# Channel mixing in two 64-row halves, placed between the score matmuls of each pair of heads

## The chip, the cores and the metric

The kernel runs on one core of one Trainium2 chip. The metric is the device time of one execution in microseconds (us), as the median of several runs. The engines are named as the profile names them: PE is the matrix engine and PEld its weight loads, DVE the vector engine, ACT the scalar engine with its activation functions, POOL the general engine, SP the engine that issues most DMAs. Every engine works through its own instructions in program order and waits on semaphores for the others. PSUM is the memory that matmuls write to.

## What is computed

Cosine attention over 8 batches, 12 heads, 448 positions and 64 elements a head, then a mixer block on the attention's output. Cut to what matters:

```
q_n, k_n = q / (norm(q) + 1e-6), k / (norm(k) + 1e-6)
attn = softmax(q_n @ k_n.T / tau) @ v                  # per head
x    = attn as [8, 448, 768]                           # heads side by side
u    = x + (relu(x.T @ w_tok1) @ w_tok2).T             # token mixing, 448 -> 256 -> 448
out  = u + relu(u @ w_ch1) @ w_ch2                     # channel mixing, 768 -> 1536 -> 768
```

## The kernel before, in words

**The work.** The attention is cut into 48 pairs of heads: 8 batches of 6 pairs. For pair i, `squares` (POOL), `norm_sum` (DVE), `norm_root` (two small ACT instructions), `norm_rec` (two small DVE instructions) and `normalize` (POOL) give normalised q and k in fp16, and `tpose_dma` lets a DMA of SP's queue transpose them into `qkT`. `score(i, g)` (L261) then makes two of the four score tiles of the pair: for each tile two matmuls, one per head, of 64 rows each, in the lower and the upper half of the array's rows; they write the two banks of a tile `pS`, of which there are two. `expo` (L268, ACT) takes the exponential of one score tile. `pv(i - 1, half)` (L282) multiplies the previous pair's exponentials by v: 24 small matmuls for the first three token tiles and 8 for the last; DVE divides by the sums (L288, L289).

**The mixer of a batch** is a list of jobs. `tok1` (L313; relu on ACT, L316) and `tok2` (L326 and, for the token tile that two batches share, L331; DVE adds x, L335) are the token mixing, called "front". When both halves of a token tile of u are there, it is cast to fp16, by DVE for tiles 1 and 5 (`recast`, L127) and by ACT for the others (L341), and a DMA transpose on SP's queue (L342) writes it to `uT`. `ch1(ct)` (L381) is the first channel mixing: 6 matmuls, each over all token tiles of `uT`, 384 columns in even batches and 512 in odd ones, and a relu on ACT into `gT` (L384). `ch2(i, dh)` (L397) is the second: 12 matmuls of 128 rows by 384 columns that add up in one PSUM tile `pF`, which DVE then adds to u (L401); `store` sends a finished token tile out.

**The order.** Slots 0 to 12 (`opening`) have an order of their own. From slot 13 on, `slot(i)` issues: squares, score group 0 and its two exponentials, `fill`, the norm's sum and root, `pv` first part, `fill`, score group 1 and its two exponentials, `fill`, the norm's reciprocal, normalisation and transpose, the cast of v, `fill`, `pv` second part, `fill`. Each `fill` takes mixer jobs from the list `todo` as far as a credit allows; `spread` sets that credit so that the jobs of a batch last six slots. After every sixth slot a new mixer is made: its front is interleaved with the `ch2` jobs (`held`) of the mixer before, and its `ch1` jobs follow. The tiles pR, pU, pG, pF and pO all come from one PSUM pool `ps` of four buffers, given out in turn: a fifth tile waits until the first was read. After slot 48 only mixer work is left.

Of the kernel before, what the change touches and what calls it, by code (L numbers as in the profile page):

```python
# [9 lines left out]
FP32 = mybir.dt.float32  # L10
FP16 = mybir.dt.float16
AF = mybir.ActivationFunctionType
ALU = mybir.AluOpType
# [5 lines left out]
def _bcast_free(ap: bass.AP, n: int) -> bass.AP:  # L19
    return bass.AP(tensor=ap.tensor, offset=ap.offset, ap=list(ap.ap) + [[0, n]])  # L20
# [3 lines left out]
def kernel(  # L24
# [19 lines left out]
    nc = tc.nc  # L44
# [7 lines left out]
    DT, CT, TT = D // 128, C // 128, T // 128  # L52
    DH = 384
    NDH = D // DH
    NPAIR = H // 2
# [8 lines left out]
    mix = ctx.enter_context(tc.tile_pool(name="mix", bufs=1))  # L64
    ps = ctx.enter_context(tc.tile_pool(name="ps", bufs=4, space=bass.MemoryType.PSUM))
# [5 lines left out]
        name=nc.get_next_instruction_name(), act_func_set_id=ACT_SET_LN_EXP,  # L71
# [18 lines left out]
    wc2t = cst.tile([128, CT, D], FP16, name="wc2t")  # L90
# [65 lines left out]
    N = len(pairs)  # L156
# [25 lines left out]
    def small(i, nm):  # L182
        if nm not in st_[i]:
            st_[i][nm] = att.tile([P, 2, 2 * NCH], FP32, name=nm, tag=nm)
        return st_[i][nm]
# [3 lines left out]
    def norm_sum(i, j=BOTH):  # L189
        nc.vector.tensor_reduce(out=small(i, "ssq")[:, j], in_=st_[i]["sq"][:, j], axis=AXX.X,  # L190
                                op=ALU.add)

    def norm_root(i, j=BOTH):
        nc.scalar.activation(out=small(i, "ln")[:, j], in_=small(i, "ssq")[:, j], func=AF.Ln)
        nc.scalar.activation(out=nns[i % 3][:, j, :, 0], in_=small(i, "ln")[:, j], func=AF.Exp,
                             scale=0.5)
# [29 lines left out]
    def tpose_dma(i):  # L226
        s = st_[i]
        s["T"] = att.tile([128, 2, S], FP16, name="qkT", tag="qkT")
        nc.sync.dma_start_transpose(
            out=s["T"][:].rearrange("d j (c p) -> d (j c) p", c=NCH),  # L230
            in_=s["qkn"][:].rearrange("p j c g e -> p (j c g e)"))
# [34 lines left out]
    def expo(i, c):  # L266
        s = st_[i]
        nc.scalar.activation(out=s["p"][:, c], in_=s["pS"][c][:, :, 0:S], func=AF.Exp,  # L268
                             scale=inv_tau)

    def pv(i, half):
        b, pj = pairs[i]
        s = st_[i]
        xt = x16[b // 2]
        d0 = 2 * pj * E
        ts = (3,) if half else (0, 1, 2)
        pO = ps.tile([128, len(ts), 2, E + 1], FP32, name="pO", tag="ps")
        for n, t in enumerate(ts):
            c0 = 128 * t if t < 3 else S - 128
            for h in range(2):  # L280
                for c in range(NCH):
                    nc.tensor.matmul(pO[:, n, h, :], s["p"][:, c, h, c0:c0 + 128],  # L282
                                     s["v16"][:, NCH * h + c, 0:E + 1],
                                     start=(c == 0), stop=(c == NCH - 1))
        m0, hp = (64, 64 * (b % 2)) if half else (0, 0)
        nr, t0 = 128 - m0, (3 if half else 4 * (b % 2))
        rec = att.tile([128, len(ts), 2], FP32, name="rec", tag=f"rec{half}")
        nc.vector.reciprocal(out=rec[m0:128], in_=pO[m0:128, :, :, E])  # L288
        nc.vector.tensor_tensor(  # L289
            out=xt[hp:hp + nr, t0:t0 + len(ts), d0:d0 + 2 * E].rearrange(  # L290
                "p t (h e) -> p t h e", h=2),
            in0=pO[m0:128, :, :, 0:E], in1=_bcast_free(rec[m0:128], E), op=ALU.mult)
# [4 lines left out]
    def mixer(b):  # L297
        e, g = b % 2, b // 2
        xt = x16[g]
        t0, nt = (0, 3) if e == 0 else (3, 4)  # L300
        W = nt * 128
# [1 line left out]
        u32 = mix.tile([128, nt, D], FP32, name="u32", tag="u32", bufs=2)  # L303
        u16 = mix.tile([128, nt, D], FP16, name="u16", tag="u16")
        uT = mix.tile([128, DT, W], FP16, name="uT", tag="uT")
        gT = mix.tile([128, CT, W], FP16, name="gT", tag="gT")

        def tok1(tt, dh):
            def job():
# [76 lines left out]
        def ch1(ct):  # L386
            return 6 * W / 2400, partial(ch1_part, ct, 0, DT)

        def ch2(i, dh):
            def job():  # L390
                end = b == B - 1 and i == t0 + nt - 1
                parts = 2 if end and dh == NDH - 1 else 1
                for z in range(parts):
                    cols = slice(dh * DH + z * DH // parts, dh * DH + (z + 1) * DH // parts)
                    pF = ps.tile([128, DH // parts], FP32, name="pF", tag="ps")
                    for ct in range(CT):
                        nc.tensor.matmul(pF[:], gT[:, ct, (i - t0) * 128:(i - t0 + 1) * 128],  # L397
                                         wc2t[:, ct, cols],
                                         start=(ct == 0), stop=(ct == CT - 1))
                    o = u32[:, i - t0, cols]  # L400
                    nc.vector.tensor_tensor(out=o, in0=pF[:], in1=o, op=ALU.add)  # L401
                    if end:
                        store(i, cols, end)
                if dh == NDH - 1 and not end:
                    store(i, slice(0, D), end)
            return 1.96, job

        def store(i, cols, end):
            if i == 3:
                parts = [(h, 64 * h, S - 64, 64) for h in range(2)]  # L410
            else:
                f0 = 128 * (i % 4)
                parts = [(e, f - f0, f, n) for f, n in f_segments(f0, f0 + 128)]
            for z, (h, m, f, n) in enumerate(parts):
                rows = out[2 * g + h].rearrange("(p c) d -> c p d", c=NCH)
                queue = nc.scalar if end and z else nc.sync
                queue.dma_start(out=rows[f // P, f % P:f % P + n, cols],
                                in_=u32[m:m + n, i - t0, cols])

        if b == 0:  # L420
            front = (tok1_pair, tok2_pair, u_pair, ch1_part)
        else:
            front = [tok1(tt, dh) for dh in range(NDH) for tt in range(TT)]
# [4 lines left out]
    def merge(a, b):  # L428

        if not b:  # L430
            return list(a)
        r, n = [], 0
        for m, x in enumerate(b):
            while n * len(b) < (m + 1) * len(a) and n < len(a):
                r.append(a[n])
                n += 1
            r.append(x)
        return r + list(a[n:])


    todo, held, first = [], [], []
    credit, gap = [0.0], [0.0]

    def fill():
        credit[0] += gap[0]
        while todo and credit[0] > 0:
            cost, job = todo.pop(0)
            credit[0] -= cost
            job()

    AHEAD = 5
    FIRST = 2 * NPAIR + 1
# [89 lines left out]

    def slot(i):

        if i + 3 < N:
            squares(i + 3)
        if i in wide:
            wide[i]()
        if i < N:
            score(i, 0)  # L550
            expo(i, 0)
            expo(i, 1)
        fill()
        if i + 2 < N:
            norm_sum(i + 2)
            norm_root(i + 2)
        pv(i - 1, 0)
        fill()
        if i < N:
            score(i, 1)  # L560
            expo(i, 2)
            expo(i, 3)
        fill()
        if i + 2 < N:
            norm_rec(i + 2)
            normalize(i + 2, False)
            tpose_dma(i + 2)
        if i + 1 < N:
            v_cast(i + 1, i % (2 * NPAIR) == 2)
        fill()  # L570
        pv(i - 1, 1)
        fill()

    def spread(jobs, slots):
# [4 lines left out]
    for i in range(N + 1):  # L579
        if i + AHEAD < N:  # L580
            load(i + AHEAD)
        if i == 2:
            first.extend(mixer(0))
        if i < N and i % (2 * NPAIR) == 0:
            xt = mix.tile([128, 7, D], FP16, name="x16", tag="x16", bufs=2)
            x16[i // (2 * NPAIR)] = xt
            nc.vector.memset(xt[64:128, 3, :], 0.0)
        if i < FIRST:
            opening(i)
        else:  # L590
            if i == FIRST:
                normalize(i + 1, False)
                tpose_dma(i + 1)
            slot(i)
        if i == NPAIR:
            spread([(1.6, lambda: None)] + first[1][2:10], NPAIR)
            late, held = first[1][10:], first[2]
        elif i and i % NPAIR == 0:
            front, c1, c2 = mixer(i // NPAIR - 1)
            if (i // NPAIR) % 2:  # L600
                mid = merge(front, held[:-3]) + held[-3:]
            else:
                mid = front[:6] + held[:1] + front[6:9] + held[1:2] + front[9:] + held[2:]
            spread(late + mid + c1, NPAIR)
            late = []
            held = c2
    for _, job in todo + held:
        job()

# [34 lines left out]
```

## Time and profile before

| | |
|---|---|
| three runs | 401.47, 403.29 and 405.5 us; median 403.29 |
| the profiled execution | 402.3 us; its span, first to last instruction, 400.5 us |
| mean granted TensorE clock | 0.996 |
| busy | PE 379.6, ACT 263.8, DVE 233.0, POOL 194.6 us |
| first `pF` matmuls / last score group / last matmul starts about | 83 / 338.9 / 397 us of the span |

In the lines of the profile, "L261 PE MATMUL pS<-qkT 64*112 64x448 f16" is a matmul of line 261 that writes pS from qkT, with weights of 64 rows and 112 columns and a moving operand of 64x448. Behind the number of instructions stand the busy time and the mean duration of one in ns. In a timeline a row holds equal instructions that follow each other: start, length from the first start to the last end, engine, line, shapes, count. Matmuls are pipelined, so a length overlaps with the next row; the time that a row takes on PE is read from its start to the start of the next one.

### The profile page before, as it was taken

What the parts mean: (1) busy time and instruction counts of PE and PEld (TensorE: products, weight loads), DVE (VectorE), ACT (ScalarE), POOL (GpSimd) and SP (SyncE); (2) the same over time, 40 slices, a digit from 0 to 9 for tenths busy, and PEclk for the clock granted to TensorE, in tenths of its full rate; (3) what the DMA queues carried; (4) which work ended last, traced back from release to release, by engine and by line L of the source; (5) the groups of instructions that cost most, each with busy time, mean ns of one, the idle gap of its engine ahead of it and who ended that gap; (6) DMA issues with size and microseconds to landing.
All of it is one profiled execution on the core that took longest, in us unless ns stands there. A gap on an engine that the chain in (4) does not pass through costs nothing.

```text
span 400.5 us, 9027 instructions
## 1 busy us (share of the span) xinstructions
PE 379.6 (95%) x3604; PEld 218.0 (54%) x3604; DVE 233.0 (58%) x531; ACT 263.8 (66%) x455; POOL 194.6 (49%) x205
## 2 busy tenths in 40 slices
PE   2788999899999999999999999999999999999996
PEld 1455656455445555555445565565555555655454
DVE  5879988576544865467544765557634763161022
ACT  6799899864876657866677557776686666522400
POOL 3989989827454547444744546544744520000000
PEclk9989999999999999999999999999999999999999
DMA  8999999967943797548863698547971452035014
GB/s 221 252 260 248 202 268 253 246 154 192 232 96 93 174 214 205 156 117 174 220 173 92 153 186 243 132 115 175 252 161 41 77 135 77 2 78 120 0 41 118
DMA packets 97465, 63.57 MB, mean 159 GB/s; under 512 B 57552, under 2 KB 93968, under 8 KB 97424
## 3 DMA queue, kind: packets, MB, share of 16 engines
q1 hardware_dynamic: 94048, 58.14, 59.7%
q0 software_dynamic: 3184, 4.72, 6.7%
q8 instruction: 28, 0.46, 0.5%
q10 hardware_dynamic: 192, 0.15, 0.1%
q14 instruction: 13, 0.11, 0.1%
HBM read 43.38 MB, written 11.01 MB: 136 GB/s over the span
## 4 chain that ended last, share of the span: by engine, by line
PE 84%; DVE 9%; ACT 4%; DMA 1%; issue 1%
PE pF L397 28%; PE pG L381 27%; PE pO L282 10%; PE pS L261 10%; PE pR L313 5%; PE pU L326 3%; DVE ssq L190 3%; ACT pE L268 2%; DVE x L289 2%; DVE qkT L248 1%; DVE u L370 1%; PE pU L331 1%; DMA ql<-in_q_dram 1%; DVE rec L288 1%; DVE rn L202 0%
## 5 line engine op out<-in xcount | busy, mean ns | idle before, releaser
L268 ACT ACTIVATE pE<-pS 112x896 f16<-112x896 f32 x192 | 164.9, 913 | 34.4 <-PE pS L261 33.8
L381 PE MATMUL pG<-uT,wc1t 128*128 128x384 f16 (+1 forms) x576 | 120.3, 353 | 0.0
L397 PE MATMUL pF<-wc2t,gT 128*128 128x384 f16 (+1 forms) x684 | 116.7, 324 | 0.5 <-DVE u L335 0.2
L213 POOL TENSOR_TENSOR qkn<-ql,rn 112x512 f16<-112x512 f32 x47 | 49.0, 1043 | 126.7 <-DVE rn L202 115.5
L397 PEld LDWEIGHTS <-gT 128*128 128x128 f16 x684 | 64.0, 98 | 46.7 <-issue 6.5
L384 ACT ACTIVATE gT<-pG 128x384 f16<-128x384 f32 (+1 forms) x96 | 52.3, 547 | 43.6 <-PE pG L381 42.6
L381 PEld LDWEIGHTS <-wc1t 128*128 128x128 f16 x576 | 51.4, 98 | 50.5 <-issue 9.3
L401 DVE TENSOR_TENSOR u<-pF,u 128x384 f32<-128x384 f32 (+1 forms) x57 | 31.3, 549 | 69.2 <-PE pF L397 69.1
L261 PE MATMUL pS<-qkT 64*112 64x448 f16 x384 | 59.9, 382 | 8.3 <-DVE qkT L248 4.2
L282 PEld LDWEIGHTS <-pE 112*128 112x128 f16 x1536 | 57.8, 99 | 16.8 <-issue 6.6
L282 PE MATMUL pO<-v,pE 112*128 112x65 f16 x1536 | 62.2, 195 | 0.0
L190 DVE TENSOR_REDUCE ssq<-sq 112x16 f32<-112x1024 f32 (+1 forms) x50 | 58.5, 1171 | 4.4 <-ACT sq L178 3.3
L288 DVE RECIPROCAL rec<-pO 128x6 f32<-128x6 f32 x96 | 17.5, 182 | 72.8 <-PE pO L282 71.8
L180 POOL TENSOR_TENSOR sq<-ql 112x512 f32<-112x512 f32 x46 | 47.8, 1038 | 5.9 <-DMA ql<-in_q_dram 5.9
L213 POOL TENSOR_TENSOR qkn<-kl,rn 112x512 f16<-112x512 f32 x47 | 49.0, 1042 | 0.0
L180 POOL TENSOR_TENSOR sq<-kl 112x512 f32<-112x512 f32 x46 | 47.8, 1038 | 0.0
L289 DVE TENSOR_TENSOR x<-pO,rec 128x384 f16<-128x384 f32 x96 | 40.9, 426 | 3.3
L261 PEld LDWEIGHTS <-qkT 64*112 64x112 f16 x384 | 18.9, 127 | 34.9 <-issue 23.8
L335 DVE TENSOR_TENSOR u<-pU,x 128x384 f32<-128x384 f32 x50 | 25.4, 545 | 8.6 <-PE pU L331 8.5
L341 ACT CAST u<-u 128x768 f16<-128x768 f32 x18 | 15.0, 832 | 19.7 <-DVE u L335 19.7
L127 DVE TENSOR_REDUCE v<-vl 112x512 f16<-112x512 f32 x40 | 25.5, 640 | 0.0
L313 PE MATMUL pR<-x,w1t 128*128 128x384 f16 x112 | 20.4, 327 | 0.0
(43 smaller groups left out, 169.8 us busy)
## 6 DMA issues: line engine op xcount, KB each, us to landing
ql<-in_q_dram SPq DMA_DIRECT2D x48, 224.0 KB, 3.7
kl<-in_k_dram SPq DMA_DIRECT2D x48, 224.0 KB, 3.8
vl<-in_v_dram SPq DMA_DIRECT2D x48, 224.0 KB, 4.1
out_dram<-u SPq DMA_DIRECT2D x8, 336.0 KB, 3.3
wc1t<-in_moe_w_ch_dram POOLq DMA_DIRECT2D x4, 576.0 KB, 8.1
wc2t<-in_moe_w_ch_dram POOLq DMA_DIRECT2D x3, 768.0 KB, 10.6
out_dram<-u SPq DMA_DIRECT2D x8, 288.0 KB, 3.7
out_dram<-u SPq DMA_DIRECT2D x7, 240.0 KB, 3.2
```

Of the source, the lines that this page charges most:

```text
L180: nc.gpsimd.tensor_mul(out=s["sq"][:, j], in0=a, in1=a)
L190: nc.vector.tensor_reduce(out=small(i, "ssq")[:, j], in_=st_[i]["sq"][:, j], axis=AXX.X, op=ALU.add)
L213: eng.tensor_tensor(out=t[:, j].rearrange("p c g e -> p g c e"), in0=s[nm][:], in1=_bcast_free(rn, E), op=ALU.mult)
L261: nc.tensor.matmul(pS[:, h, 0:S], s["T"][64 * h:64 * h + 64, 1, c * P:(c + 1) * P], s["T"][64 * h:64 * h + 64, 0, :], start=True, stop=True)
L268: nc.scalar.activation(out=s["p"][:, c], in_=s["pS"][c][:, :, 0:S], func=AF.Exp, scale=inv_tau)
L282: nc.tensor.matmul(pO[:, n, h, :], s["p"][:, c, h, c0:c0 + 128], s["v16"][:, NCH * h + c, 0:E + 1], start=(c == 0), stop=(c == NCH - 1))
L289: nc.vector.tensor_tensor(out=xt[hp:hp + nr, t0:t0 + len(ts), d0:d0 + 2 * E].rearrange("p t (h e) -> p t h e", h=2), in0=pO[m0:128, :, :, ...
L313: nc.tensor.matmul(pR[:], w1t[:, wi, tt * 128:(tt + 1) * 128], xt[:, xi, dh * DH:(dh + 1) * DH], start=(n == 0), stop=(n == 3))
L381: nc.tensor.matmul(pGs[ct][:], wc1t[:, dt, ct * 128:(ct + 1) * 128], uT[:, dt, :], start=(dt == 0), stop=(dt == DT - 1))
L384: nc.scalar.activation(out=gT[:, ct, :], in_=pGs[ct][:], func=AF.Relu)
L397: nc.tensor.matmul(pF[:], gT[:, ct, (i - t0) * 128:(i - t0 + 1) * 128], wc2t[:, ct, cols], start=(ct == 0), stop=(ct == CT - 1))
L401: nc.vector.tensor_tensor(out=o, in0=pF[:], in1=o, op=ALU.add)
```

## The change

It has four parts.

- `ch2` can run split: each of its 12 matmuls becomes two of 64 rows, one in each half of the array's rows, into two `pF` tiles; DVE adds both to u, one after the other. A token tile is stored when both of its column halves are done, counted in `seen`.
- The six (for the first mixer five) first `ch2` jobs of a batch leave the list and wait in `halves`. From slot 14 on each slot takes one of them, split, between score group 0 and score group 1; the last (slot 48, without scores) runs unsplit. The tile `gT` gets a second buffer.
- The order in a slot: `norm_sum` comes ahead of score group 0; the first `fill` is gone from between the score groups; `pv` and all fills come after score group 1, and the norm's reciprocal, normalisation and transpose after two of these fills.
- The list of a batch is now: the whole front, then `ch2` jobs that are left (two of an odd batch, one of the first, none of the other even ones), then an empty job with a cost of 3.0 or 0.8, then `ch1`.

In program order this makes 34 slots (14 to 47) of the form "4 score matmuls, 24 half matmuls of pF, 4 score matmuls", and in slot 13 the 8 score matmuls follow each other directly. Behind the last pU matmul of a batch PE then has: for batches 3 and 5, which end their front in slots 26 and 38, only the next slot's scores, 24 half matmuls and the 24 matmuls of pv before the first pG; for batches 2, 4 and 6 (slots 20, 32, 44) two whole `ch2` jobs more.

```
-        gT = mix.tile([128, CT, W], FP16, name="gT", tag="gT")
+        gT = mix.tile([128, CT, W], FP16, name="gT", tag="gT", bufs=2)
...
         def ch2(i, dh):
-            def job():
+
+            def job(split=False):
...
+                rows = (slice(0, 64), slice(64, 128)) if split else (slice(0, 128),)
...
-                    pF = ps.tile([128, DH // parts], FP32, name="pF", tag="ps")
+                    pFs = [ps.tile([128, DH // parts], FP32, name="pF", tag="ps") for _ in rows]
                     for ct in range(CT):
-                        nc.tensor.matmul(pF[:], gT[:, ct, (i - t0) * 128:(i - t0 + 1) * 128],
-                                         wc2t[:, ct, cols],
-                                         start=(ct == 0), stop=(ct == CT - 1))
+                        for pF, k in zip(pFs, rows):
+                            nc.tensor.matmul(pF[:], gT[k, ct, (i - t0) * 128:(i - t0 + 1) * 128],
+                                             wc2t[k, ct, cols],
+                                             start=(ct == 0), stop=(ct == CT - 1))
                     o = u32[:, i - t0, cols]
-                    nc.vector.tensor_tensor(out=o, in0=pF[:], in1=o, op=ALU.add)
+                    for pF in pFs:
+                        nc.vector.tensor_tensor(out=o, in0=pF[:], in1=o, op=ALU.add)
...
     def slot(i):
...
+        if i + 2 < N:
+            norm_sum(i + 2)
         if i < N:
             score(i, 0)
             expo(i, 0)
             expo(i, 1)
-        fill()
+        if halves and i > FIRST:
+            halves.pop(0)[1](split=i < N)
         if i + 2 < N:
-            norm_sum(i + 2)
             norm_root(i + 2)
-        pv(i - 1, 0)
-        fill()
         if i < N:
             score(i, 1)
             expo(i, 2)
             expo(i, 3)
+        pv(i - 1, 0)
+        fill()
+        pv(i - 1, 1)
+        fill()
         if i + 2 < N:
             norm_rec(i + 2)
             normalize(i + 2, False)
             tpose_dma(i + 2)
+        fill()
         if i + 1 < N:
             v_cast(i + 1, i % (2 * NPAIR) == 2)
         fill()
-        pv(i - 1, 1)
         fill()
...
-            if (i // NPAIR) % 2:
-                mid = merge(front, held[:-3]) + held[-3:]
+            if i < N:
+                n = NPAIR - (i < FIRST)
+                halves.extend(held[:n])
+                mid = front + held[n:] + [(0.8 if i // NPAIR % 2 else 3.0, lambda: None)]
             else:
```

More of the change, by code (lines that the diff above doesn't have):

```diff
@@ L387, in ch1 @@
             return 6 * W / 2400, partial(ch1_part, ct, 0, DT)
+        seen = []
         def ch2(i, dh):
-            def job():
+            def job(split=False):
                 end = b == B - 1 and i == t0 + nt - 1
                 parts = 2 if end and dh == NDH - 1 else 1
+                rows = (slice(0, 64), slice(64, 128)) if split else (slice(0, 128),)
                 for z in range(parts):
                     cols = slice(dh * DH + z * DH // parts, dh * DH + (z + 1) * DH // parts)
-                    pF = ps.tile([128, DH // parts], FP32, name="pF", tag="ps")
+                    pFs = [ps.tile([128, DH // parts], FP32, name="pF", tag="ps") for _ in rows]
                     for ct in range(CT):
-                        nc.tensor.matmul(pF[:], gT[:, ct, (i - t0) * 128:(i - t0 + 1) * 128],
-                                         wc2t[:, ct, cols],
-                                         start=(ct == 0), stop=(ct == CT - 1))
+                        for pF, k in zip(pFs, rows):
+                            nc.tensor.matmul(pF[:], gT[k, ct, (i - t0) * 128:(i - t0 + 1) * 128],
+                                             wc2t[k, ct, cols],
+                                             start=(ct == 0), stop=(ct == CT - 1))
                     o = u32[:, i - t0, cols]
-                    nc.vector.tensor_tensor(out=o, in0=pF[:], in1=o, op=ALU.add)
+                    for pF in pFs:
+                        nc.vector.tensor_tensor(out=o, in0=pF[:], in1=o, op=ALU.add)
                     if end:
                         store(i, cols, end)
-                if dh == NDH - 1 and not end:
+                seen.append(i)
+                if seen.count(i) == NDH and not end:
                     store(i, slice(0, D), end)
@@ L438, in merge @@
         return r + list(a[n:])
-    todo, held, first = [], [], []
+    todo, held, first, halves = [], [], [], []
     credit, gap = [0.0], [0.0]
@@ L604 @@
             spread(late + mid + c1, NPAIR)
-            late = []
-            held = c2
+            late, held = [], c2
     for _, job in todo + held:
```

## The prediction

> **What bounds the kernel now.** I read the page first, then busy time by stages, then PE's timeline of one slot, then DVE and ACT where a batch's last u is made.
>
> ```profile
> PE 379.6 (95%) x3604; PEld 218.0 (54%) x3604; DVE 233.0 (58%) x531; ACT 263.8 (66%) x455; POOL 194.6 (49%) x205
> ...
> PE 84%; DVE 9%; ACT 4%; DMA 1%; issue 1%
> ```
>
> ```profile
> 213.30:258.50 45.20, 45.20 (x440) 26.44 (x439) 28.85 (x67) 30.74 (x54) 24.27 (x25) 1.00 0.71 171
> ```
>
> The page's chain that ended last is 84% PE. The second fence is the stage view of one batch: 45.20 us long, PE (first pair of numbers) busy in all of it, ACT (fourth) 30.74, granted clock 1.00. The view of PE's waits for the time after 94 us is empty. So from there on PE's queue is the time: what it spends less is gain, and any wait put into it is loss.
>
> PE's timeline, four rows of one slot, then two of the next:
>
> ```profile
> 253.59 1.14 PE L381 MATMUL pG<-uT,wc1t 128*128 128x384 f16 x6
> 254.66 0.59 PE L261 MATMUL pS<-qkT 64*112 64x448 f16 x4
> 255.18 2.12 PE L381 MATMUL pG<-uT,wc1t 128*128 128x384 f16 x12
> 257.14 0.41 PE L282 MATMUL pO<-v,pE 112*128 112x65 f16 x8
> ...
> 260.28 0.89 PE L282 MATMUL pO<-v,pE 112*128 112x65 f16 x24
> 261.01 1.30 PE L313 MATMUL pR<-x,w1t 128*128 128x384 f16 x7
> ```
>
> From start to start, 12 pG take 1.96, 0.163 each. The 6 before the scores take 1.07, not 0.975: 0.095 to enter the 64-row form. Four score matmuls run as two pairs of 448 columns; two times 0.163 x 448/384 = 0.38, but the row takes 0.52: 0.14 too much (0.045 for the first weights, 0.09 to leave); the single records show 0.012 more at the first full matmul. Changing form and back costs **0.24 us**, twice a slot.
>
> **The change, part by part**
>
> *Form changes.* Slots 14 to 47 have row-half pF between the score groups, and slot 13 has them back to back: 35 returns go, 35 x 0.24 = **-8.4 us**, if a pair of half matmuls is as quick as one whole matmul. The trace has no 64-row x 128-column weights. The nearest rows:
>
> ```profile
> 254.66 0.18 PEld L261 LDWEIGHTS <-qkT 64*112 64x112 f16 x4 [0.32 <-issue]
> ```
>
> ```profile
> 171.55 0.84 PE L331 MATMUL pU<-r,w2t 128*64 128x384 f16 x8
> 172.33 0.50 PE L397 MATMUL pF<-wc2t,gT 128*128 128x384 f16 x2
> ```
>
> All four weight loads of a score group are over 0.18 after the first began, while the first pair still streams. Four pairs in column halves take 0.78 with entry and exit costs of about 0.12 in it, 0.165 a pair. Bounds for a row pair: 0.163 (nothing) to 0.163 + 0.045 (a score pair's first load in each): 0 to 0.045 x 12 x 34 = +18 us. I take 0, by the pU row.
>
> [...]
>
> *Ordinary slots.* The second score group needs both pS tiles back from ACT.
>
> ```profile
> 9.52 1.72 ACT L268 ACTIVATE pE<-pS 112x896 f16<-112x896 f32 x2
> 10.49 0.62 PE L261 MATMUL pS<-qkT 64*112 64x448 f16 x2 [0.64 <-ACT pE L268]
> 11.29 0.62 PE L261 MATMUL pS<-qkT 64*112 64x448 f16 x2 [0.19 <-ACT pE L268]
> ```
>
> ```profile
> 258.56 0.49 ACT L384 ACTIVATE gT<-pG 128x384 f16<-128x384 f32 x1 [0.73 <-PE pG L381]
> 258.94 1.72 ACT L268 ACTIVATE pE<-pS 112x896 f16<-112x896 f32 x2
> ```
>
> Two exponentials take 1.72 (second 0.80 after the first), and PE's next pair starts 0.05 after the one that frees its tile. In the second fence scores start at 258.45: exponentials from 0.50, even behind a relu, done at 2.21, so the last pair could start at 2.26. PE gets to it at 0.42 (first group) + 12 x 0.163 + 0.19 = 2.57. **0**, with a margin of 0.31.
>
> *Slot 13.* No pF there: last pair due at 0.61, possible at 2.26: **+1.65**.
>
> *Slots with a batch's last u.* Before, whole pF stood between the pU; now they stand close together, DVE falls behind, and ACT's cast of u waits for DVE with the next slot's exponentials queued behind it, for which PE waits.
>
> ```profile
> 179.88 0.19 DVE L288 RECIPROCAL rec<-pO 128x6 f32<-128x6 f32 x1
> 180.10 0.56 DVE L289 TENSOR_TENSOR x<-pO,rec 128x384 f16<-128x384 f32 x1
> 180.58 0.55 DVE L335 TENSOR_TENSOR u<-pU,x 128x384 f32<-128x384 f32 x1
> 181.16 0.95 DVE L127 TENSOR_REDUCE u<-u 128x768 f16<-128x768 f32 x1
> 182.03 0.55 DVE L335 TENSOR_TENSOR u<-pU,x 128x384 f32<-128x384 f32 x1
> ```
>
> ```profile
> 183.40 0.83 ACT L341 CAST u<-u 128x768 f16<-128x768 f32 x1 [0.82 <-DVE u L335]
> 184.14 1.72 ACT L268 ACTIVATE pE<-pS 112x896 f16<-112x896 f32 x2
> ```
>
> Steps: rec 0.22, x 0.48, add 0.47 (0.58 ahead of a recast), recast 0.87, 64-row rec 0.21 and x 0.32. Slots 26 and 38, from E, when PE leaves pv's 24 matmuls: rec at 0.20 (261.01 to 261.21 in the trace), add(5,1) 1.37, recast 1.95, add(6,0) 2.82, second rec 3.28, add(6,1) 3.81 to 4.36. Cast 4.39; v's cast, in these slots on ACT (0.62 in the groups, about 0.5 to the next), 5.13; exponentials 5.63 to 7.35; last score pair 7.40. PE: six pU 0.98, pv's 8 0.24, two pU 0.33, entry 0.09, then 2.57: due at 4.20. **+3.2** each. The transposes of u take 2.7 to 5.9 to land (DMA view, median 3.1): cast over at 5.22, uT at 8.0 to 8.4, while pG is reached at 7.40 + 0.28 + 0.71 = 8.39: hidden, but with nothing to spare (up to +2.8 each by the slowest landing).
>
> Slots 25 and 37, same steps: pU starts at E + 2.84, v's cast holds DVE until 3.2, add(4,1) ends 5.43, cast 5.46, exponentials 6.22 to 7.94, last pair 7.99 instead of 7.00: **+1.0** each. So +4.2 for batch 3 and for batch 5.
>
> Batches 2, 4, 6: add(0,1) ends at E + 4.39, cast, exponentials 5.18 to 6.90; last pair 6.95 instead of 6.48: +0.5. A slot later pU and pF find the four ps buffers full (DVE's x and adds 0.16 and 0.13 late): +0.3. Two whole pF jobs (3.9) then cover the cast and the transposes, with 0.9 left. **+0.8** each.
>
> Batch 1 (slot 14): ten pU behind pv, buffers 0.75 late in all; cast and v's cast make the next exponentials late by 0.8: **+1.6**.
>
> *The rest* costs nothing. 34 more additions of 0.556 are 3.3 us a batch on DVE, which by the stage view has 16 us free in 45 and, in the slots above, is through with pF at E. 408 more matmuls and loads: a pair of pv's instructions passes in 0.03, so four in 0.06 of 0.163. norm_sum goes earlier on DVE (its squares are a slot old). norm_rec, POOL's normalisation (2 x 1.04) and SP's transpose (2.7) come later, yet land near 10 after the slot began (reciprocals over at 5.3 behind pv's last x, 2.1 on POOL, 2.7 to land) and are wanted two slots on, at 11.7 or more (shortest slot: 2.87 to the end of the scores, pv 0.95, twelve pG 1.95, entry 0.09, so 5.86); u's transposes stand ahead of that transpose on SP's queue in slots 20, 26 and so on, the loads behind it are five slots early, the stores wait for DVE only. The second gT buffer only takes a wait away.
>
> **Sum:** -8.4 + 1.65 + 1.6 + 2 x 4.2 + 3 x 0.8 = **+5.6 us** on the profiled 402.3, so 407.9; the median of the runs is 1.0 above that execution, so 408.9.
>
> **The rivals**
>
> *DVE keeps up and u's casts hold nothing (faster).* Only slot 13 and batch 1's buffers stay: -8.4 + 2.4 = -6.0, 397.3. It needs add(6,1) 3.2 us sooner in slots 26 and 38. For it: DVE is 42% idle. Against: it is in order, and the chain above is back to back from rec on.
>
> *Waits half as long (same).* 7.0 against 8.4: 401.9. For it: waits can overlap in ways I counted twice, and E itself moves when a buffer is late. Against: the largest one is a single chain.
>
> *Loads of half weights exposed (slower).* +18, of which the late casts hide about a fifth: near 423.
>
> *The form change stays (the change doesn't do what it says).* If pS to pF in halves drains too, 0 is gained: 403.3 + 14.0 = 417.3. Both are 64-row forms, differing in columns only.
>
> **How the numbers follow.** Chances: forecast 0.58 (own range 405 to 415, the top by slow landings), faster rival 0.14, halved waits 0.18, exposed loads 0.06, no gain 0.04. Range 399 to 416: leaves out most of the faster rival and both dear ones. About 1%, 4 us, is what a measurement can tell from no change. Slower: 0.50 of the forecast, 0.06, 0.04 and 0.01 of the halved waits, 0.61. Faster: 0.12 and 0.01, 0.13. Same: 0.26.
>
> **What would show it.** Right: 24 half pF in 1.96 to 2.0 us between score groups, no 0.09 at either side; PE waits on ACT's pE of about 3 us in slots 27 and 39, about 1 in 26 and 38, 1.65 in slot 13. Wrong: rows of 24 longer than 2.2; score waits after every slot (the 0.31 margin was too thin); pG waiting for uT; or no waits at all.

## The result, and the profile after

The changed kernel takes 417.69 us (median of six runs, 413.67 to 419.7) beside 402.48 for the kernel before on the same chip: ratio 1.037, 95% interval 1.033 to 1.042. It is slower, as forecast, but by about 15 us and not by 5.6.

The six runs differ by their granted clock: 413.67 us at 0.992, 416.53 and 416.66 at 0.984, 418.72, 419.36 and 419.7 at 0.980. The profiled execution is the first of these, with a span of 411.9 us, 11.4 more than before; so the trace shows the mildest case, and the spread is part of the result. The ratios leave out executions more than 1.5% above the fastest of the same kernel (two of e2's four, one of e4's four, two of six in e5 and in e7, one each in e6 and e8, none of the changed kernel's six), which flatters e2, e4 and e7 a little beside it, and the traces of e2 and e7 are of executions left out.

From the page of the changed kernel, to be held against the lines shown of before:

```profile
PE 381.0 (92%) x4012; PEld 224.0 (54%) x4012; DVE 254.8 (62%) x565; ACT 268.6 (65%) x455; POOL 194.8 (47%) x205
...
PEclk9999999898999999999999999999999999999999
...
PE 75%; DVE 14%; ACT 8%; DMA 2%; issue 1%
```

PE is as long busy as before, but of a longer span: 92% instead of 95%. The chain that ended last now leads through DVE and ACT for 22% (13% before). And two slices of the granted clock read 8.

PE's timeline of slot 25, then of slot 27 (start, length, engine, line, names, shapes, count, idle before and who ended it):

```profile
172.75 0.59 PE L261 MATMUL pS<-qkT 64*112 64x448 f16 x4
173.17 2.11 PE L402 MATMUL pF<-wc2t,gT 64*128 64x384 f16 x24
175.12 0.54 PE L261 MATMUL pS<-qkT 64*112 64x448 f16 x4
175.60 0.90 PE L282 MATMUL pO<-v,pE 112*128 112x65 f16 x24
...
187.31 0.59 PE L261 MATMUL pS<-qkT 64*112 64x448 f16 x4
187.74 0.32 PE L402 MATMUL pF<-wc2t,gT 64*128 64x384 f16 x1
188.82 2.11 PE L402 MATMUL pF<-wc2t,gT 64*128 64x384 f16 x23 [0.76 <-DVE u L335]
192.14 0.40 PE L261 MATMUL pS<-qkT 64*112 64x448 f16 x2 [1.21 <-ACT pE L268]
192.94 0.40 PE L261 MATMUL pS<-qkT 64*112 64x448 f16 x2 [0.41 <-ACT pE L268]
```

In slot 25 the form changes are gone as planned: scores to pF 0.42, 24 half matmuls from 173.17 to 175.12 = 1.95, which is 12 x 0.1625 and the pace of 12 whole ones (1.96 for 12 pG of 384 columns in the kernel before), and straight on into the scores. 29 of the 34 groups of 24 take 1.95 from their start to the next scores; the other five stand among waits. In slot 27 the last score pair starts 5.63 after the first, where 2.56 would do: 3.07 of waits.

Their cause on DVE and ACT in the changed kernel:

```profile
189.33 0.56 DVE L335 TENSOR_TENSOR u<-pU,x 128x384 f32<-128x384 f32 x1
```

```profile
189.92 0.83 ACT L341 CAST u<-u 128x768 f16<-128x768 f32 x1 [3.68 <-DVE u L335]
...
191.18 1.72 ACT L268 ACTIVATE pE<-pS 112x896 f16<-112x896 f32 x2
```

DVE's last addition of u ends at 189.89; ACT, which had idled for 3.68, casts u, then v (0.61, the line left out), and only then takes slot 27's exponentials, whose scores had been ready since about 187.8.

What no line before showed is the clock. Busy time by stretches (us, then PE, PEld, DVE, ACT, POOL busy, then the granted clock, DMA share and GB/s):

```profile
71.70:75.10 3.40, 1.08 (x9) 0.53 (x8) 2.13 (x4) 2.99 (x5) 3.36 (x4) 1.00 1.13 234
75.10:78.50 3.40, 3.40 (x32) 2.15 (x32) 0.75 (x2) 1.83 (x3) 1.20 (x2) 0.50 1.39 262
95.60:99.00 3.40, 1.47 (x34) 1.15 (x33) 2.09 (x8) 2.15 (x5) 0.52 (x1) 1.00 0.79 164
99.00:102.40 3.40, 3.27 (x8) 1.20 (x9) 1.63 (x2) 0.49 (x1) 3.36 (x4) 0.50 0.81 269
```

Behind each of the two stretches of 3.4 us in which PE was busy for 1.08 or 1.47 stands one with a granted clock of 0.50, in which PE is busy for 3.40 and 3.27. In the second the 12 pG take 4.30 (99.12 to 103.42), in slot 27 2.68 (195.71 to 198.39): 1.62 lost. Half of the busy time, an estimate for both, is about 1.65 us each. The two at half clock begin 23.9 us apart and last 3.41 us each. The first is slot 13, whose waits stand behind one that the kernel before had too (1.09 for `qkT`); the second is slot 15, where the first pG waits for `uT`:

```profile
99.12 4.37 PE L381 MATMUL pG<-uT,wc1t 128*128 128x512 f16 x12 [1.78 <-DMA uT<-u]
```

```profile
94.15 1.22 SPq L229 DMA_TRANSPOSE qkT<-qkn  x1
95.47 1.24 SPq L342 DMA_TRANSPOSE uT<-u  x1
```

The cast was over at 93.67, but on SP's queue the transpose of u stood behind that of the next `qkT`, which had waited for POOL; it was issued 1.8 later. In slot 39 the first pG waits as well:

```profile
282.00 4.46 SPq L342 DMA_TRANSPOSE uT<-u  x2
288.73 1.46 PE L381 MATMUL pG<-uT,wc1t 128*128 128x512 f16 x6 [0.88 <-DVE x L289]
```

The first of the two transposes takes 3.1 of the 4.46 to issue, so the second is issued at 285.2, 0.8 after its cast, and lands 3.4 later, at 288.6. The view names DVE's x, but in slot 27 the same pG starts at 194.17, ahead of that x (194.44).

### The profile page after: what moved, and what is told of

It reads as the page before. It is cut to its first block, busy times and chain, and to the rows that moved or that the text cites. A ratio compares the mean times of both kernels' runs of the same rounds, so it can differ in the third digit from the quotient of the medians.

```text
span 411.9 us, 9929 instructions
## 1 busy us (share of the span) xinstructions
PE 381.0 (92%) x4012; PEld 224.0 (54%) x4012; DVE 254.8 (62%) x565; ACT 268.6 (65%) x455; POOL 194.8 (47%) x205
## 4 chain that ended last, share of the span: by engine, by line
PE 75%; DVE 14%; ACT 8%; DMA 2%; issue 1%
PE pG L381 26%; PE pF L402 22%; PE pO L282 11%; PE pS L261 8%; ACT pE L268 5%; PE pR L313 4%; DVE u L335 3%; DVE ssq L190 2%; DVE x L289 2%; PE pU L326 2%; ACT u L341 2%; DVE qkT L248 2%; DVE u L370 1%; DMA uT<-u 1%; DVE rec L288 1%
## 5 line engine op out<-in xcount | busy, mean ns | idle before, releaser
L402 PE MATMUL pF<-wc2t,gT 64*128 64x384 f16 (+2 forms) x1092 | 116.9, 322 | 1.5 <-DVE u L335 1.5
L407 DVE TENSOR_TENSOR u<-pF,u 128x384 f32<-128x384 f32 (+1 forms) x91 | 50.3, 553 | 101.7 <-PE pF L402 98.2
L402 PEld LDWEIGHTS <-gT 64*128 64x128 f16 (+1 forms) x1092 | 66.6, 95 | 46.5 <-issue 3.6
L381 PEld LDWEIGHTS <-wc1t 128*128 128x128 f16 x576 | 53.4, 99 | 49.0 <-issue 3.4
L261 PE MATMUL pS<-qkT 64*112 64x448 f16 x384 | 60.8, 380 | 14.9 <-ACT pE L268 8.9
L282 PEld LDWEIGHTS <-pE 112*128 112x128 f16 x1536 | 55.2, 99 | 19.7 <-issue 14.3
L261 PEld LDWEIGHTS <-qkT 64*112 64x112 f16 x384 | 22.8, 129 | 41.2 <-issue 27.1
## 6 DMA issues: line engine op xcount, KB each, us to landing
wc2t<-in_moe_w_ch_dram POOLq DMA_DIRECT2D x3, 768.0 KB, 10.1
```

What stands on the lines that cost most here:

```text
L261: nc.tensor.matmul(pS[:, h, 0:S], s["T"][64 * h:64 * h + 64, 1, c * P:(c + 1) * P], s["T"][64 * h:64 * h + 64, 0, :], start=True, stop=True)
L381: nc.tensor.matmul(pGs[ct][:], wc1t[:, dt, ct * 128:(ct + 1) * 128], uT[:, dt, :], start=(dt == 0), stop=(dt == DT - 1))
L402: nc.tensor.matmul(pF[:], gT[k, ct, (i - t0) * 128:(i - t0 + 1) * 128], wc2t[k, ct, cols], start=(ct == 0), stop=(ct == CT - 1))
```

## The experiments

**e1, the ch2 jobs between the scores left whole**

```
-            halves.pop(0)[1](split=i < N)
+            halves.pop(0)[1](split=False)
```

> The changed kernel with the ch2 jobs between the score groups left whole (12 matmuls of 128 rows). Theory (each return from the 64-row form to the full one costs 0.24 us, and the halves themselves cost nothing): 34 returns come back, +8.2 us, of which some 1.5 are hidden where PE waits for exponentials anyway, so about 6.5 us over the changed kernel; no gap in PE's timeline around the scores other than 0.09 at each change of form. Rival (the halves are what costs, by twice the instructions, twice the DVE additions and two PSUM tiles instead of one): faster than the changed kernel by several us.

Measured: 420.93 us, ratio to the kernel before 1.046 (1.036 to 1.055), the changed kernel 1.037. So the halves do not cost several us, as the rival had it; but the gain of some 3 us is half of what was expected, and the intervals overlap. Its profiled execution has more half clock (by its mean of 0.978 over 421.1 us an estimated 18.5 us of it, beside 6.8 in the trace of the changed kernel) and shorter waits for uT (1.1 beside 1.95 and 1.04), so it says little on the size. e9 repeats it on cleaner ground.

**e2, pv between the score groups where no ch2 job is (slot 13)**

```
+        own = bool(halves) and i > FIRST
+        if own:
             halves.pop(0)[1](split=i < N)
+        else:
+            pv(i - 1, 0)
+            fill()
...
+        if own:
+            pv(i - 1, 0)
+            fill()
```

> The changed kernel, but where a slot has no ch2 job to put between its score groups (slot 13) it puts pv's first part and a fill there, as before. Theory: the two waits of PE on the exponentials in slot 13 (0.98 + 0.57 us in the changed kernel) go, and with them the half clock from 75.1 to 78.5 us; one return of 0.24 comes back: 1.3 us less without the clock, up to 3.0 less with it. Rival (the clock falls by itself, not because PE idled): 1.3 us less, and a half clock near 75 us stays.

Measured: ratio 1.026 (1.017 to 1.036), about 4.5 us less than the changed kernel, but from two executions only (410.5 and 414.94 us; the other two took 418). In its trace slot 13 has no waits for exponentials any more, and what follows runs at full pace: 24 matmuls of pv take 0.75 us there (77.50 to 78.25), in the changed kernel 1.31 (75.56 to 76.87, at 0.50). That a wait of 1.6 us was worth more than itself fits the theory, but these runs do not show it.

**e3, ACT's casts of u on POOL**

```
-                        nc.scalar.copy(out=u16[:, i - t0, :], in_=u32[:, i - t0, :])
+                        nc.gpsimd.tensor_copy(out=u16[:, i - t0, :], in_=u32[:, i - t0, :])
```

> The changed kernel with the casts of u that ACT made given to POOL. Theory (the exponentials were late because they stood behind the cast in ACT's queue): PE's waits for exponentials in slots 20, 26, 32, 38 and 44 go, but in slots 27 and 39 the first pG then waits for uT instead, for u is late by itself (DVE's last addition 4.36 us after pv, then a cast and 2.7 us of transpose): waits of 0.6 to 1 us fewer in five slots, the 3 us of slots 27 and 39 only change their name; 2 to 4 us less in all. Rival (the late exponentials alone are the cost): all of these waits go, 9 us less or more.

Measured: ratio 1.030 (1.023 to 1.037), about 3 us less. PE's waits from slot 12 on in this kernel (who waited for whom, us in total, times, longest):

```profile
PE pG L381 <- DMA uT<-u: 9.1, 3, 3.4
...
PE pS L261 <- ACT pE L268: 1.0, 2, 0.8
```

In the changed kernel the same view has 6.5 us of ACT pE and 1.8 of uT. The exponentials no longer wait (the 1.0 left is slot 13), and uT takes their place: in slots 27 and 39 the first pG is late by 3.6 and 3.0, and in slot 15 by 3.1 instead of 1.95. So the queue behind the cast decided where PE stood still, not whether: u itself is late.

**e4, idle stretches filled with matmuls that nobody reads**

```
+    def idle_work(n):
+        pD = ps.tile([128, 256], FP32, name="pD", tag="ps")
+        for _ in range(n):
+            nc.tensor.matmul(pD[:], w1t[:, 0, 0:128], w1t[:, 0, :], start=True, stop=True)
...
+        if i in AFTER:
+            idle_work(AFTER[i])
         if i + 2 < N:
             norm_root(i + 2)
```

> The changed kernel with added matmuls whose result nobody reads, put where PE waits: 8 in slot 13 between the score groups, 5 + 16 in slot 15, 9 + 12 in slots 27 and 39 (256 columns, about 0.11 us each). Nothing that is computed is left out. Theory (PE's idle stretches of 2 to 3 us let the clock fall to one half for 3.4 us at a time, which costs about 1.7 us of work each): the granted clock goes from 0.98-0.992 to 0.99 and above in every run, and the time falls by 2 to 6 us although work is added. Rival (the clock falls for another reason): clock as in the changed kernel, time the same or longer by what the added matmuls overrun, 0 to 2 us.

Measured: ratio 1.025 (1.019 to 1.030), about 5 us less than the changed kernel, with 71 matmuls more. Granted clocks 0.991, 0.992, 0.996 and, in the execution of 419.3 us, 0.988, instead of 0.980 to 0.992: better, but "0.99 and above in every run" was missed once. The same stretches of this kernel's trace, slots 13 and 15:

```profile
73.90:77.30 3.40, 2.15 (x20) 1.18 (x17) 2.32 (x5) 3.00 (x5) 3.36 (x4) 1.00 1.14 241
77.30:80.70 3.40, 3.24 (x46) 2.28 (x46) 1.41 (x5) 2.53 (x6) 1.42 (x2) 1.00 1.39 258
97.00:100.40 3.40, 3.27 (x52) 2.66 (x51) 2.25 (x8) 1.62 (x3) 0.51 (x1) 1.00 0.71 177
```

PE's busy share rises and the clock stays at 1.00, also in the 3.4 us that follow the third (PE busy for 3.40). The mean of 0.991 over 410.6 us leaves an estimated 7.4 us at half clock elsewhere in this execution; where they lie is not shown. From slot 13's first score matmul to the last matmul this execution takes 331.9 us and the changed kernel's profiled one 335.7. That useless work makes the kernel faster is what only the clock theory foresaw.

**e7, the cast of token tiles 1 and 5 from DVE to POOL**

```
-                        recast(u16[:, i - t0, :], u32[:, i - t0, :])
+                        nc.gpsimd.tensor_copy(out=u16[:, i - t0, :], in_=u32[:, i - t0, :])
```

> The changed kernel with the cast of token tiles 1 and 5, which DVE makes between the additions of u, given to POOL. Theory (slots 27 and 39 wait because DVE's chain of additions is long): the chain is shorter by 0.87 + 0.11, so in slots 27 and 39 the waits of PE fall from 2.9 to about 1.9 us, and POOL has tile 5 ready before it is needed; 2 to 3 us less in all, more if half-clock stretches go. Rival (ACT or the PSUM buffers set these waits, not DVE): waits as in the changed kernel.

Measured: ratio 1.030 (1.028 to 1.032), about 3 us less. In slot 27 the last score pair comes 4.64 after the first, 0.99 sooner than in the changed kernel, as the chain of DVE foretold. But the first pG then waits 0.96 for its input, where it hardly waited before: in that slot nothing is won, and where the 3 us come from its trace does not show. The chain of additions sets the score waits; behind it stands the transpose.

**e5 and e6, the late u covered.** Both take e2's slot and keep more ch2 jobs whole for odd batches; e6 puts them all behind the front,

```
-                n = NPAIR - (i < FIRST)
+                n = len(held) - (3 if i < FIRST else 2)
                 halves.extend(held[:n])
-                mid = front + held[n:] + [(0.8 if i // NPAIR % 2 else 3.0, lambda: None)]
+                mid = front + held[n:] + [(0.8, lambda: None)]
```

e5 puts one of them in the middle of the front, and makes token tile 1 first in even batches:

```
+                mid = front[:8] + held[n:n + 1] + front[8:] + held[n + 1:] + [(0.8, lambda: None)]
...
-            front += [tok2(i, dh) for i in range(t0, t0 + nt) for dh in range(NDH)]
+            front += [tok2(i, dh) for i in ((3, 4, 5, 6) if e else (1, 0, 2)) for dh in range(NDH)]
```

> The changed kernel with three things altered: without a ch2 job a slot puts pv's first part and a fill between its score groups; for odd batches two more ch2 jobs stay whole (three for the first); of the whole jobs one stands in the middle of the front and the others behind it, and even batches make token tile 1 first. 29 slots keep their row halves. Theory: 29 x 0.24 = 7.0 us of form changes gone, some 3 us of waits left (the ones in slots 25 to 27 and 37 to 39 are under cover), clock as in the kernel before: 1 to 5 us less than before, near 397. Rival (the new order costs by itself, in clock or in waits elsewhere): not under 405.

> Between the changed kernel and e5: pv between the score groups where no ch2 job is, and two more whole ch2 jobs for odd batches (three for the first), but all of them behind the front. Theory: the late cast of slots 26 and 38 is under 3.9 us of pF, so the 2.9 us of waits before the scores of slots 27 and 39 and the pG waits for uT go; the waits for the cast one slot earlier stay (0.6 in slots 26, 38; 0.3 in 20, 32, 44); 28 to 29 returns saved, 7.0 us; no half clock after 80 us: 398 to 402. Rival (the waits only move to another place): 408 or more.

Measured: e5 ratio 1.018 (1.016 to 1.021), e6 1.000 (0.998 to 1.002; 402.05 us, the profiled span 399.8 beside 400.5). e5 missed, as its rival had it: with 28 split jobs, not 29, pG waits 0.9 to 2.0 us for uT in five places. A whole job in the middle of the front makes the last u later and leaves only one behind it; the new order of the token tiles, the other difference from e6, was not tried alone. e6 landed at the upper end of what was expected. Its waits from slot 12 on:

```profile
PE pS L261 <- ACT pE L268: 1.6, 6, 0.4
PE pS L261 <- DVE qkT L248: 1.1, 1, 1.1
PE pS L261 <- DMA qkT<-qkn: 1.0, 1, 1.0
```

and its granted clock in the profile is 1.0. Two whole pF jobs behind the last u of an odd batch, and pv in slot 13, take away the whole loss of the change.

**e9, e6 with the jobs between the scores whole**

> e6 with its 28 ch2 jobs between the score groups left whole: what the row halves alone are worth where hardly any wait covers for them. Theory: 28 x 0.24 = 6.7 us more than e6, about 1 of it hidden in e6's waits for exponentials (each is shorter when the scores come 0.24 later): 5 to 7 us more, near 408. Rival (the halves pay for what they save with twice the instructions, DVE additions and PSUM tiles): within 2 us of e6.

The edit is that of e1. Measured: 407.77 us, ratio 1.014 (1.009 to 1.018), that is 5.4 us more than e6 by the ratios (each to the kernel before on its own chip; the two ran on different ones) and 5.5 by the profiled spans (405.3 and 399.8, clocks 0.999 and 1.0). One slot of it in PE's timeline:

```profile
196.00 0.59 PE L261 MATMUL pS<-qkT 64*112 64x448 f16 x4
196.52 2.12 PE L402 MATMUL pF<-wc2t,gT 128*128 128x384 f16 x12
198.58 0.58 PE L261 MATMUL pS<-qkT 64*112 64x448 f16 x4
199.09 1.15 PE L282 MATMUL pO<-v,pE 112*128 112x65 f16 x32
```

From the first score to pv 3.09 us; with halves (slot 25 above) 2.85. The 0.24 of the prediction is there, and 28 of them are worth 5.4 where few waits hide them. It also shows what is left of the loss: without the halves the new order is 1.4% slower than the kernel before, so in e6 the halves only make up for it.

**e8, e6 with ACT's casts on POOL and one more half for the first batch**

> e6 (two whole ch2 jobs behind the front of odd batches, pv between the score groups where no ch2 job is) with the casts of u that ACT made given to POOL, and one row half more for the first batch. Theory (what is left in e6 are waits for exponentials behind ACT's casts, 0.5 twice and 0.3 three times, and 0.9 in slot 18): these 2.9 us go, u still lands under cover of the two whole jobs: 399 to 400, 2 us less than before. Rival (POOL's casts hold its squares and normalisations, and qkT comes late): 402 or more, with PE waiting for qkT.

Measured: 404.77 us, ratio 1.005 (1.001 to 1.008): no gain. The score waits behind casts are gone, but with only two whole jobs the first batch's pG waits 2.5 for uT, another one 1.3, and a score 1.5 for qkT, as the rival had it. No version beat the kernel before.

## Why the prediction was wrong

**Form changes, -8.4: right.** 0.24 a slot; row-half pairs as quick as whole matmuls (1.95 for 24), so the "0" taken from the column-half row held, and the dear rival with exposed weight loads and the rival in which the form change stays are both refuted by the trace, although the latter's 417.3 lies near the time measured. Where waits do not cover it, e9 measures 5.4 for 28 slots, against 6.7 by the same sum, of which about 1 was expected to be hidden.

**Waits behind late casts, +14.05: right.** By the last score pair's start against when it was due: slot 13 1.61 (predicted 1.65); slots 25 to 26 0.83 (1.0); slots 26 to 27 3.07 (3.2), and the same in 38 and 39; 0.32 in each even batch (0.5); slot 15 1.11 (0.8). With the short waits at the PSUM buffers (0.9 in slot 14, about 0.28 in each batch from 2 to 6) 13.8. Ordinary slots wait for nothing, as said.

**uT "hidden, but with nothing to spare": the first step that failed.** In slot 39 it landed later (the transpose of tile 5 ahead of it on SP's queue took 3.1 to issue), and pG waited 1.04. In slot 15 it was 1.95, by the queue: I had checked SP's order for slots 20 and 26, not for slot 14, where u's last transpose stands behind `qkT`. Together +3.0 for which the sum had 0, though the text gave up to +2.8 as a bound for each of slots 27 and 39; for slot 15 it had none.

**The clock: the step that was not there.** The sum priced every wait at its own length, at a granted clock of 1.00 throughout. In the profiled execution two stretches at half clock (0.50 for 3.41 us from 75.10 and from 99.00) cost an estimated 3.3 us more; with them and uT the sum is -8.4 + 13.8 + 3.0 + 3.3 = 11.7, and the trace has 12.0 from slot 13 to the last matmul. The median is another 4.0 above this execution; uT, the clock and these 4.0 are, within 1 us, what lies between the 5.6 forecast and the 15.2 measured. In the other five runs the clock was 0.980 to 0.984 instead of 0.992: if all that is missing stands at 0.50, as in this trace, a mean of 0.980 over 417 us is 16.7 us of half clock, against 6.6 in the profiled run, so 10.1 us more, an estimated 5.0 us lost if PE is busy all through them; the times differ by 5 to 6. That in the profiled execution it is PE's idle stretches, and not something else in the change, is what e4 (the stretches of slots 13 and 15 filled, the clock 1.00 in them, about 5 us less) and e6 (most waits gone, mean clock 1.0, 402.05 us) speak for. For the other executions the cause is open: no trace shows where their half clock lies. Part may lie in the opening, which the change does not touch: the trace of the kernel before has 3.41 us at 0.50 there (25.03 to 28.44), that of the changed kernel shows none, and of the 41 executions of the kernel before whose clock was recorded beside the experiments three are at 0.983 to 0.987. Part may be where stretches of 3.41 us fall against the waits, a guess that no run tests: laid end to end from the half clock of this trace, two of them share slot 39's waits, with 1.79 and 2.53 us of matmuls, and the clock stays at 1.00; in e1 a stretch of 3.40 us (290.10 to 293.50) has 0.94, and 3.40 us at 0.51 follow.

Which waits cost the clock is not settled by these traces. In the changed kernel no single gap of PE from slot 13 on was longer than 1.78 us, and yet half clock followed stretches of 3.41 us with 1.09 and 1.47 us of matmuls in them. No sharp limit comes out: the stretch with 1.79 in slot 39 kept the clock at 1.00, and in the opening of the kernel before one with 1.79 (21.62 to 25.03) stands ahead of 3.41 us at 0.50. In e8 PE waited 2.5 us at one place in an execution with a mean clock of 1.0.

**The rivals.** "DVE keeps up" is refuted by the chain above: DVE's last addition of slot 26 starts 3.94 after PE leaves pv's 24 matmuls, where 3.81 was predicted. "Waits half as long" is refuted by the 13.8. The forecast's range ended at 416 because it took slow landings as the only way up.

## What to carry to other kernels

When PE is the bound and has no gaps, any wait put into it costs its length (here -8.4 + 13.8 + 3.0 + 3.3 = 11.7 stand beside the 12.0 of the trace) and may cost the clock: here half clock followed two 3.41 us stretches with 2.32 and 1.94 us without matmuls, for an estimated 1.65 us more each. Ask for the clock around each wait, and check how the median's clock differs from the profiled run's. A job that is taken away from between a producer chain and its consumer is also cover that is taken away: before moving it, follow the chain through every in-order queue (here DVE's additions, ACT's cast ahead of the exponentials, SP's transposes) to the next thing that PE needs. Moving a late step to another engine mostly moved the wait, where its consumer was as late (about 3 us gained in e3 and e7, none in e8); giving it cover removed it (e6).

## What the runs showed of the hardware

- In the changed kernel 24 matmuls of 64 rows in the two row halves of the array (weights of 128 columns, 384 columns each) took 1.95 us from their start to the next scores in 29 of 34 groups, 0.1625 a pair; in the kernel before 12 matmuls of 128 rows by 384 columns took 1.96. From the first of four 64-row score matmuls to them passed 0.42, to full ones 0.52 (before and e9); from their first to the next scores 1.95, from that of 12 full ones 2.06 (e9).
- With the changed kernel's trace divided into stretches of 3.41 us from its own half clock, a granted clock of 0.50 for 3.41 us followed those at 1.00 with PE busy for 1.09 and 1.47 us. It did not follow one with 1.79 us (283.37 to 286.78); in the kernel before it followed one with 1.79 us (21.62 to 25.03). In e1 6.80 us at 0.50 followed 3.50 us at 0.99 with 1.32 us of matmuls, and 3.40 us at 0.51 followed 3.40 us at 0.99 with 0.94.
- A cast of 128x768 from fp32 to fp16 took 0.82 us on POOL (e3 and e7), 0.83 on ACT and 0.95 on DVE (before).
